# A banded attention with a feed-forward layer: value steps set directly ahead of score steps, and two tails woven into groups 3 and 5

## The chip, the cores and the metric

The kernel runs on one core of a Trainium2 chip. The metric is the device time of one execution in microseconds (us), taken as the median of several runs; lower is better. The engines of the core work through their own queues in program order and wait for each other through semaphores: PE (matmul, with PEld for the loads of its weights), DVE (vector), ACT (scalar), POOL (GpSimd) and SP, which only issues DMAs here.

## The reference

```python
# q, k, v: 8 batches x 8 heads x 576 positions x 64, float32
scores = q @ k^T / sqrt(64)
mask = (0 <= i - j) & (i - j < 64)          # a causal window of 64
attn = softmax(where(mask, scores, -1e9))
x = concat_heads(attn @ v)                  # 8 x 576 x 512
xn = (x - mean(x)) / sqrt(var(x) + 1e-6) * g_ln
out = x + relu(xn @ w_ch1) @ w_ch2          # w_ch1 512 x 2048, w_ch2 2048 x 512
```

All inputs and the output are float32; the kernel works with float16 operands in its matmuls.

## The kernel before, in words

The work is cut into nine groups. Groups 0 to 7 are positions 0 to 511 of one batch each, in four blocks (kb) of 128 positions. Group 8 holds the tails: positions 512 to 575 of all batches, two batches to a block, so four tail blocks, numbered by i. For each group the kernel does the feed-forward part (the MLP) of group g on PE while it prepares the attention of batch b = g + 1, loads and casts batch n = g + 2, and does one or two of the tails (TAILS: group 3 does tail 0, group 5 tail 1, group 7 tails 2 and 3).

The order is written out by hand. mlp_units returns a list of units, each a run of matmuls. Group 1 has 32 units: 16 of layer 1 (l1_half, L537, eight matmuls of 256 columns) and 16 of layer 2 (L413, four of 512). From group 2 on there are 30: units 0 to 15 are layer 1 (L401, four matmuls of 128x512 each), units 16 to 29 are layer 2 (L478, eight of 128x256 each: a Strassen-like scheme with seven products of two halves). In it DVE makes sums of the hidden layer (s_sums, L452). at(i, f, ...) puts a step into slot i, and the main loop emits unit i, then the steps of slot i in the order in which at was called. Since every engine's queue keeps the order of emission, a step's slot decides what stands ahead of it on each engine.

The steps of a block's attention are:

- cast_qk (L128, POOL) turns q or k of half a batch into float16. t_main then transposes it. From batch 3 on, q goes by a DMA transpose that SP issues (L223). k goes through PE (L229) and ACT, which copies the result to qkT (L215).
- s_mm (score step): 16 matmuls of 64 rows (L286) into two PSUM buffers sc; ACT takes their exponential (L294) into pt.
- s_mask: DVE multiplies pt by the window's mask (L301).
- b_step (value step): 16 matmuls of 64 columns (L321), which read pt and the float16 copies vA and vB of v, into the one buffer xps. DVE divides (L324, L327) and makes mean and variance (L329, L332, tile mvg).
- z_step: POOL normalises in four instructions (L351 to L354, tiles rsz and z). In groups 0 and 1 DVE does it instead, and newton (L380 to L390), a run of twelve small DVE instructions, makes the factors.
- zt_step: z is transposed to zT, the next MLP's input; mostly by a DMA that SP issues (L362), for block 3 of batches 3 and 5 by PE (L366).

For v, cast_v (L147, POOL) makes vA, and make_vB (L165, L166) copies it shifted by half a block with two DMAs that POOL issues. cast_tail (L117 to L120) and t_tail (L248, L257) do the like for a tail. The loads of batch n + 1 (load_qk L94, load_v L141) are issued by SP at the end of the group, those of a tail (load_tail, L106 to L108) in slot 1.

Buffers that matter here: two sc, one xps, two for PE's transposes, two for MLP sums (mm), two float16 buffers each for q and k, three z, four pt.

Before the change the steps of batch b in groups 2 to 6 sit in these slots: value steps 2, 7, 12, 17; score steps of blocks 1 to 3 in slots 2, 7, 12, each behind a value step; the score step of block 0 of batch n in slot 27. A tail of group 3 or 5 has its score step in slot 1, its value step in slot 5. In group 1 the score steps of batch 2 sit in 9, 13, 16, 19 and its value steps in 14, 17, 20, 23.

Of the kernel before, what the change touches and what calls it, by code (L numbers as in the profile page):

```python
# [20 lines left out]
def kernel(  # L21
# [11 lines left out]
    B, H, S, D = q.shape  # L33
# [3 lines left out]
    NGRP = B + 1  # L37
# [4 lines left out]
    XQ = 3  # L42
# [802 lines left out]
    TAILS = {3: [0], 5: [1], 7: [2, 3]}  # L845
    for g in range(NGRP):
        if g == NGRP - 1:
            for _ in rest:
                pass
            break  # L850
        units, s_sums = mlp_units(g, (8, 16)[g] if g < 2 else 0, g == 0, g > 1)
        slots = [[] for _ in range(len(units) + 1)]

        def at(i, f, *a):
            slots[min(i, len(slots) - 1)].append((f, a))

        b = g + 1
        if g == 0:
            at(0, b_step, 0, 3)
            at(1, zt_step, 0, 2)  # L860
            at(3, zt_step, 0, 3, "dve")
            at(4, newton, 0, 0, 4)
            at(11, t_main, 1, 0, 0, 1)
            at(12, t_main, 1, 1, 0, 1)
            at(13, vB_cur, 1, 0, 1)
            at(13, vB_prev, 1, 0, 1)
            at(13, vB_cur, 1, 1, 1)
            at(13, vB_prev, 1, 1, 1)
            at(16, s_mm, 1, 0)
            at(16, s_mask, 1, 0)  # L870
            at(17, s_mm, 1, 1)
            at(17, s_mask, 1, 1)
            at(18, b_step, 1, 0)
            at(20, b_step, 1, 1)
            at(21, zt_step, 1, 0)
            at(23, zt_step, 1, 1)
            at(24, t_main, 1, 0, 1, 0)
            at(26, t_main, 1, 1, 1, 1)
            at(25, vB_cur, 1, 2, 0)
            at(25, vB_prev, 1, 2, 1)  # L880
            at(26, vB_cur, 1, 3, 0)
            at(28, s_mm, 1, 2)
            at(28, s_mask, 1, 2)
            at(30, s_mm, 1, 3)
            at(30, s_mask, 1, 3)
            at(27, load_v, 2, 0, 4)
        if g == 1:
            at(0, cast_qk, 2, 0)
            at(0, cast_qk, 2, 1)
            at(0, b_step, 1, 2)  # L890
            at(2, b_step, 1, 3)
            at(3, zt_step, 1, 2)
            at(13, newton, 1, 0, 4)
            at(6, zt_step, 1, 3)
            at(4, alloc_v, 2)
            at(4, alloc_qkT, 2)
            at(4, alloc_vB, 2)
            at(5, cast_v, 2, 0, 4)
            at(5, make_vB, 2)
            at(4, t_main, 2, 0, 0)  # L900
            at(4, t_main, 2, 1, 0)
            at(6, t_main, 2, 0, 1)
            at(6, t_main, 2, 1, 1)
            at(7, w2_sums, 3, 0, 4)
            at(8, w2_sums, 3, 4, 8)
            at(25, w2_sums, 2, 0, 4)
            at(28, w2_sums, 2, 4, 8)
            for j in range(4):
                at((9, 13, 16, 19)[j], s_mm, 2, j)
                at((10, 14, 17, 20)[j], s_mask, 2, j)  # L910
                at((14, 17, 20, 23)[j], b_step, 2, j)
                at((14, 17, 20, 23)[j], z_step, 2, j)
                at((18, 21, 24, 27)[j], zt_step, 2, j)
            at(3, load_qk, 3, 0)
            at(4, load_qk, 3, 1)
            at(7, load_v, 3, 0, 4)
            at(8, alloc_qkT, 3)
            at(8, cast_qk, 3, 0)
            at(10, cast_qk, 3, 1)
            at(14, alloc_v, 3)  # L920
            at(14, cast_v, 3, 0, 2)
            at(14, cast_v, 3, 2, 4)
            at(17, alloc_vB, 3)
            at(17, make_vB, 3)
            at(31, s_mm, 3, 0)
            at(31, s_mask, 3, 0)
            for i, (x, half) in zip((12, 24, 12, 28), ((0, 0), (1, 0), (0, 1), (1, 1))):
                at(i, t_main, 3, x, half, 0)
            at(40, load_qk, 4, 0)
            at(40, load_qk, 4, 1)  # L930
            at(40, load_v, 4, 0, 4)
        if g == 2:
            for m, i in enumerate((1, 4)):
                at(4 + 2 * m, w2_sums, i, 0, 4)
                at(5 + 2 * m, w2_sums, i, 4, 8)
        if g > 1 and g + 2 < B:
            at(11, alloc_qkT, g + 2)
            if g + 2 >= XQ:
                at(11, cast_qk, g + 2, 0, (0,))
                at(11, cast_qk, g + 2, 1, (0,))  # L940
                at(11, cast_qk, g + 2, 0, (1,))
            else:
                at(11, cast_qk, g + 2, 0)
        if g > 1 and b < B:
            for j in range(4):
                if j:
                    at((2, 7, 12)[j - 1], s_mm, b, j)
                    at((3, 8, 13)[j - 1], s_mask, b, j)
                at((2, 7, 12, 17)[j], b_step, b, j)
                at((2, 7, 12, 17)[j], z_step, b, j)  # L950
                at((12, 12, 18, {3: 24, 5: 23}.get(b, 22))[j], zt_step, b, j)
        for n, i in enumerate(TAILS.get(g, ())):
            ts = (13, 13, 17, 22) if n else (1, 2, 5, 11)
            at(ts[0], s_mm, NGRP - 1, i)
            at(ts[1], s_mask, NGRP - 1, i)
            at(ts[2], b_step, NGRP - 1, i)
            at(ts[2], z_step, NGRP - 1, i)
            at(ts[3], zt_step, NGRP - 1, i)
        n = g + 2
        if g > 1 and n < B:  # L960
            at(16, cast_qk, n, 1, (1,) if n >= XQ else (0, 1))
            at(20, alloc_v, n)
            at(20, cast_v, n, 0, 2)
            at(21, cast_v, n, 2, 4)
            at(21, alloc_vB, n)
            at(21, make_vB, n)
            for i, (x, half) in zip((13, 18, 13, 22) if g == 2 else (13, 17, 13, 21),
                                    ((0, 0), (1, 0), (0, 1), (1, 1))):
                at(i, t_main, n, x, half, 0)
            at(27, s_mm, n, 0)  # L970
            at(28, s_mask, n, 0)
            if n + 1 < B:
                at(40, load_qk, n + 1, 0)
                at(40, load_qk, n + 1, 1)
                at(40, load_v, n + 1, 0, 4)
        if g > 1:
            for i in range(1, 5):
                at(7 + i, s_sums, 0, 4, i)
                at(13 + i // 3, s_sums, 4, 6, i)
                at((15, 15, 19, 21)[i - 1], s_sums, 6, 8, i)  # L980
        for n, i in enumerate(TAILS.get(g + 1, ())):
            if n == 0:
                at(1, load_tail, i)
                at(24 if i < 2 else 18, cast_tail, i)
                at(27 if i < 2 else 22, t_tail, i, 0)
                at(29 if i < 2 else 22, t_tail, i, 1)
            else:
                at(25, load_tail, i)
        if len(TAILS.get(g, ())) == 2:
            at(3, cast_tail, TAILS[g][1])  # L990
            at(7, t_tail, TAILS[g][1], 0)
            at(7, t_tail, TAILS[g][1], 1)
        if g == NGRP - 2:
            at(0, w1_sums, 1, 2)
            at(3, w1_sums, 3)
            at(21, w1_sums, 4)
            at(27, z_sums, NGRP - 1, 1, 2)
            at(28, z_sums, NGRP - 1, 3, 4)
            at(27, begin_last)
            at(28, lambda: next(rest))  # L1000
        for i, u in enumerate(units):
            if i == (20 if g > 1 else 17 if g == 0 else -1):
                tbank["shared"] = True
            u()
            for f, a in slots[i]:
                f(*a)
        for f, a in slots[len(units)]:
            f(*a)
# [28 lines left out]
```

## Time and profile before

| what | value |
|---|---|
| median of 3 runs | 308.82 us (308.48 to 309.07) |
| the profiled execution | 310.37 us |
| its span, first to last instruction | 308.5 us |
| mean granted TensorE clock | 0.999 |
| PE, DVE, POOL, ACT busy | 96%, 72%, 56%, 49% of the span |
| q1, the DMA queue of SP | 73% of 16 engines' span, 54.67 MB |
| group 1 starts its layer 1 at | 55.9 us |
| group 2 | 95.1 us |
| group 3 | 126.5 us |
| group 4 | 157.8 us |
| group 5 | 189.2 us |

The page of the profile gives each engine's busy time, then the span in 40 slices, the DMA queues, the chain of work that ended last, and groups of instructions by source line. Further views are answers of the trace: who waited for whom; the timeline, with start, length, engine, line, operation and tiles of each instruction or run of them, and in brackets the idle time ahead of it with its releaser; the instructions of one tile with the time from issue to landing of the DMAs that write it; and busy time in chosen stretches. SPq is SP's issue of a DMA; its length is that of the issue and not of the transfer. Starts are counted from the span's start. Matmuls overlap in the array, so the distance from one start to the next tells what one costs; its listed length is longer.

### The profile page before, as it was taken

How to read it: one execution, taken by the hardware profiler on the slowest of the kernel's cores; microseconds unless marked ns; L12 is line 12 of the kernel's file. 1: busy time of each engine (PE TensorE's matmuls, PEld its weight loads, DVE VectorE, ACT ScalarE, POOL GpSimd, SP SyncE). 2: the span in 40 equal slices, each digit the busy share in tenths (PEclk: the TensorE clock that was granted, in tenths of full speed). 3: DMA queues.
4: the chain of work that ended last, by engine and by line, in shares of the span. 5: the costliest groups of instructions: out<-in, count | busy, mean ns of one | idle time of the engine just before them, and what ended most of it. 6: DMA issues, size and time to landing. Idle time of an engine off the chain costs nothing.

```text
span 308.5 us, 7581 instructions
## 1 busy us (share of the span) xinstructions
PE 296.3 (96%) x3061; PEld 196.6 (64%) x3061; DVE 221.2 (72%) x412; ACT 150.8 (49%) x253; POOL 172.0 (56%) x256
## 2 busy tenths in 40 slices
PE   7989999997999999999999999999999999999992
PEld 4557544686454479646964686459645864788882
DVE  0688665767784996589666965897569686689972
ACT  1486635676316742775247526762376046305500
POOL 6588676536780798369814984598337507024300
PEclk9999999999999999999999999999999999999999
DMA  8999998999856997898479997994790399003014
GB/s 190 294 360 303 305 361 242 302 282 251 151 140 191 269 208 118 254 312 157 44 215 320 195 169 206 325 142 78 213 189 19 53 178 215 19 17 138 0 37 102
DMA packets 113669, 58.35 MB, mean 189 GB/s; under 512 B 83617, under 2 KB 104609, under 8 KB 113634
## 3 DMA queue, kind: packets, MB, share of 16 engines
q1 hardware_dynamic: 112576, 54.67, 73.1%
q0 software_dynamic: 768, 2.80, 3.8%
q8 instruction: 24, 0.39, 0.5%
q10 hardware_dynamic: 290, 0.40, 0.5%
q14 instruction: 11, 0.09, 0.1%
HBM read 38.80 MB, written 9.44 MB: 156 GB/s over the span
## 4 chain that ended last, share of the span: by engine, by line
PE 81%; DVE 5%; DMA 5%; POOL 3%; ACT 2%; issue 1%; SPq 1%; POOLq 0%; ACTq 0%
PE hps L401 25%; PE pA L478 10%; PE pC L478 7%; PE pB L478 7%; PE ch L413 5%; PE hph L537 4%; PE xps L321 4%; PE ch L554 3%; PE sc L286 3%; PE tp L229 3%; DMA v<-in_v_dram 3%; PE lA L592 2%; DMA zT<-z 2%; ACT pt L294 2%; PE warm L765 2%
## 5 line engine op out<-in xcount | busy, mean ns | idle before, releaser
L401 PE MATMUL hps<-zT,w1g 128*128 128x512 f16 x416 | 95.3, 379 | 0.0
L405 ACT ACTIVATE hrT<-hps 128x512 f16<-128x512 f32 x104 | 62.2, 599 | 39.4 <-PE hps L401 35.8
L401 PEld LDWEIGHTS <-w1g 128*128 128x128 f16 x416 | 38.6, 98 | 43.3 <-issue 0.7
L294 ACT ACTIVATE pt<-sc 128x512 f16<-128x512 f32 x72 | 39.0, 595 | 28.4 <-PE sc L286 19.9
L478 PEld LDWEIGHTS <-sS 128*128 128x128 f16 x448 | 43.3, 98 | 5.0
L351 POOL TENSOR_SCALAR rsz<-mvg 128x1 f32<-128x1 f32 x28 | 10.2, 363 | 63.9 <-DVE mvg L332 63.2
L128 POOL CAST qk<-qk 128x1024 f16<-128x1024 f32 x32 | 34.5, 1096 | 10.3 <-DMA qk<-in_q_dram 5.3
L301 DVE TENSOR_TENSOR pt<-pt,mask 128x1024 f16<-128x1024 f16 x32 | 28.9, 907 | 10.3 <-ACT pt L294 10.2
L478 PEld LDWEIGHTS <-hrT 128*128 128x128 f16 x336 | 32.4, 98 | 5.5 <-ACT hrT L637 0.3
L215 ACT COPY qkT<-tp 128x1024 f16<-128x1024 f16 x16 | 16.1, 1013 | 34.2 <-PE tp L229 34.1
L485 DVE TENSOR_TENSOR xn<-pA,xn 128x512 f32<-128x512 f32 x28 | 19.2, 685 | 16.8 <-PE pA L478 11.2
L478 PE MATMUL pC<-w2s,sS 128*128 128x256 f16 x224 | 27.1, 273 | 0.0
L478 PE MATMUL pA<-wT,sS 128*128 128x256 f16 x224 | 26.9, 273 | 0.0
L354 POOL TENSOR_SCALAR z<-xn,rsz 128x512 f16<-128x512 f32 x28 | 24.8, 885 | 3.0 <-DMA zT<-z 0.2
L329 DVE BATCH_NORM_STATS2 stats<-xn 128x6 f32<-128x512 f32 x36 | 25.0, 695 | 1.2
L327 DVE TENSOR_TENSOR xn<-xps,rcp 128x512 f32<-128x512 f32 x36 | 24.9, 691 | 1.2
L324 DVE RECIPROCAL rcp<-xps 128x8 f32<-128x8 f32 x36 | 7.3, 204 | 25.1 <-PE xps L321 25.1
L452 DVE TENSOR_TENSOR sS<-hrT 128x512 f16<-128x512 f16 (+1 forms) x40 | 24.5, 612 | 0.6 <-ACT hrT L405 0.6
L537 PE MATMUL hph<-zT,w1g 128*128 128x256 f16 x192 | 23.3, 273 | 0.5 <-DVE zT L371 0.5
L321 PEld LDWEIGHTS <-pt 128*64 128x64 f16 x576 | 12.3, 110 | 15.3 <-issue 6.8
L147 POOL CAST vA<-v 128x1024 f16<-128x1024 f32 (+2 forms) x19 | 17.3, 928 | 6.1 <-DMA v<-in_v_dram 6.0
L352 POOL TENSOR_TENSOR rsz<-rsz,mhalf 128x1 f32<-128x1 f32 x28 | 19.3, 691 | 2.3
(113 smaller groups left out, 450.1 us busy)
## 6 DMA issues: line engine op xcount, KB each, us to landing
out_dram<-xn SPq DMA_DIRECT2D x33, 256.0 KB, 2.4
qk<-in_q_dram SPq DMA_DIRECT2D x16, 512.0 KB, 6.3
qk<-in_k_dram SPq DMA_DIRECT2D x16, 512.0 KB, 7.2
v<-in_v_dram SPq DMA_DIRECT2D x32, 256.0 KB, 7.2
w2s<-in_moe_w_ch_dram SPq DMA_DIRECT2D x9, 512.0 KB, 9.2
w1s<-in_moe_w_ch_dram SPq DMA_DIRECT2D x4, 512.0 KB, 8.2
tk<-in_k_dram SPq DMA_DIRECT2D x8, 256.0 KB, 4.4
tv<-in_v_dram SPq DMA_DIRECT2D x8, 256.0 KB, 5.2
```

The lines of the kernel that those rows point to most:

```text
L128: nc.gpsimd.tensor_copy(out=dst[:, :].rearrange("p (a j) e d -> p a e j d", j=j), in_=t[:, :].rearrange("p (a e j d) -> p a e j d", e=2, j ...
L294: nc.scalar.activation(out=o, in_=i, func=AF.Exp, bias=0.0, scale=scale)
L301: nc.vector.tensor_tensor(out=ptv, in0=ptv, in1=mb, op=ALU.mult)
L321: nc.tensor.matmul(out=xps[64 * r:64 * r + 64, h, :D + 1], lhsT=pt[:, par, hp, r, :], rhs=rhs, start=True, stop=True)
L327: nc.vector.tensor_tensor(out=xn, in0=xps[:, :, 0:D], in1=rcp_b, op=ALU.mult)
L329: nc.vector.bn_stats(out=stats, in_=xv)
L354: nc.gpsimd.tensor_scalar(out=z, in0=xv, scalar1=rs, scalar2=nm, op0=ALU.mult, op1=ALU.add)
L401: nc.tensor.matmul(out=hps, lhsT=w1g[:, kc, 128 * hc:128 * (hc + 1)], rhs=zT[g][:, kc, :], start=(kc == 0), stop=(kc == NKC - 1),)
L405: nc.scalar.activation(out=hrT[:, hc, :], in_=hps, func=AF.Relu, bias=0.0, scale=1.0)
L452: nc.vector.tensor_tensor(out=o, in0=x, in1=y, op=op)
L478: nc.tensor.matmul(out=o, lhsT=a[:, c, 128 * p:128 * p + 128], rhs=wv[:, c, :], start=(first and (p == 0 or split_c) and c == 0), stop=(c ...
L537: nc.tensor.matmul(out=hps[:, e], lhsT=w1g[:, kc, 128 * hc:128 * (hc + 1)], rhs=zT[g][:, kc, 256 * half:256 * half + 256], start=(kc == 0) ...
```

## The change

It moves steps between slots. No instruction is added or removed.

- Group 1 (batch 2): newton from slot 13 to 9. Score steps to 10, 13, 15, 18, value steps to 15, 18, 21, 23. Those of blocks 0 and 1 now stand directly ahead of the score steps of blocks 2 and 3. The zt_steps go to 19, 22, 25, 27.
- Groups 3 and 5 (tails): value step of block 0 in slot 2, then the tail's score step; the tail's value step in slot 6, then the score step of block 1; value step 1 and score step 2 in slot 10; value step 2 and score step 3 in slot 14; value step 3 in slot 18. The tail's zt_step goes from 11 to 14, those of batch b from 12, 12, 18, 22 to 12, 15, 20, 23.
- Group 4: value step of block 3 from slot 17 to 19, and directly behind it the first score step of batch 6, from 27. So that it can stand there, the transposes of k of batch 6 are called in slots 16 and 17 (17 and 21 before) and the cast of k's second half in slot 13 (16 before). The zt_step of block 3 goes from 23 to 24.
- Groups 2, 6 and 7 keep their slots; group 7 alone keeps the old way of doing tails.

```diff
-            at(13, newton, 1, 0, 4)
+            at(9, newton, 1, 0, 4)
...
-                at((9, 13, 16, 19)[j], s_mm, 2, j)
-                at((10, 14, 17, 20)[j], s_mask, 2, j)
-                at((14, 17, 20, 23)[j], b_step, 2, j)
-                at((14, 17, 20, 23)[j], z_step, 2, j)
-                at((18, 21, 24, 27)[j], zt_step, 2, j)
+                at((15, 18, 21, 23)[j], b_step, 2, j)
+                at((15, 18, 21, 23)[j], z_step, 2, j)
+                at((10, 13, 15, 18)[j], s_mm, 2, j)
+                at((11, 14, 16, 19)[j], s_mask, 2, j)
+                at((19, 22, 25, 27)[j], zt_step, 2, j)
...
+        n = g + 2
         if g > 1 and b < B:
+            tails = g in TAILS and n < B
+            bs = (2, 10, 14, 18) if tails else (2, 7, 12, 19 if g == 4 else 17)
+            ss = (6,) + bs[1:3] if tails else bs[:3]
+            if tails:
+                i = TAILS[g][0]
+                at(bs[0], b_step, b, 0)
+                at(bs[0], z_step, b, 0)
+                at(bs[0], s_mm, NGRP - 1, i)
+                at(bs[0] + 1, s_mask, NGRP - 1, i)
+                at(ss[0], b_step, NGRP - 1, i)
+                at(ss[0], z_step, NGRP - 1, i)
+                at(14, zt_step, NGRP - 1, i)
             for j in range(4):
-                if j:
-                    at((2, 7, 12)[j - 1], s_mm, b, j)
-                    at((3, 8, 13)[j - 1], s_mask, b, j)
-                at((2, 7, 12, 17)[j], b_step, b, j)
-                at((2, 7, 12, 17)[j], z_step, b, j)
-                at((12, 12, 18, {3: 24, 5: 23}.get(b, 22))[j], zt_step, b, j)
-        for n, i in enumerate(TAILS.get(g, ())):
+                if j or not tails:
+                    at(bs[j], b_step, b, j)
+                    at(bs[j], z_step, b, j)
+                if j < 3:
+                    at(ss[j], s_mm, b, j + 1)
+                    at(ss[j] + 1, s_mask, b, j + 1)
+                at((12, 15 if tails else 12, 20 if tails else 18, {3: 24, 4: 23, 5: 24, 6: 23}.get(b, 22))[j], zt_step, b, j)
+        for n, i in enumerate(TAILS.get(g, ()) if g == NGRP - 2 else ()):
             ts = (13, 13, 17, 22) if n else (1, 2, 5, 11)
...
-            at(16, cast_qk, n, 1, (1,) if n >= XQ else (0, 1))
+            at(13 if g == 4 else 16, cast_qk, n, 1, (1,) if n >= XQ else (0, 1))
...
-            for i, (x, half) in zip((13, 18, 13, 22) if g == 2 else (13, 17, 13, 21),
+            for i, (x, half) in zip({2: (13, 18, 13, 22), 4: (13, 16, 13, 17)}.get(g, (13, 17, 13, 21)),
                                     ((0, 0), (1, 0), (0, 1), (1, 1))):
                 at(i, t_main, n, x, half, 0)
-            at(27, s_mm, n, 0)
-            at(28, s_mask, n, 0)
+            at(19 if g == 4 else 27, s_mm, n, 0)
+            at(20 if g == 4 else 28, s_mask, n, 0)
```

## The prediction

> **What bounds the kernel now.** I read the page first (busy shares, then the chain that ended last), then the waits of PE, then the timelines of PE, POOL and SP (its DMA queue) around each edit.
>
> ```profile
> PE 296.3 (96%) x3061; PEld 196.6 (64%) x3061; DVE 221.2 (72%) x412; ACT 150.8 (49%) x253; POOL 172.0 (56%) x256
> PE 81%; DVE 5%; DMA 5%; POOL 3%; ACT 2%; issue 1%; SPq 1%; POOLq 0%; ACTq 0%
> ```
>
> PE is the bound: 96% busy, 81% of the chain. A shift of PE work can therefore gain only by taking out a wait or an overhead of PE, and every new wait of PE costs its full length. PE's waits have one large entry:
>
> ```profile
> PE xps L321 <- DVE rstmp L387: 1.7, 1, 1.7
> ```
>
> It stands at 74.65 to 76.32, before the value step of batch 2, block 0. Its mask (L301) ended at 73.95 and nothing of L387 (newton) is an input of it; so the named releaser had no part in it. The tile vB, asked for alone around 66 to 72 us, shows another:
>
> ```profile
> L165 POOL DMA_DIRECT2D vB<-vA x1: 744/744/744, 68.9 to 68.9; - x1
> DMA to landing us min/median/max: 7.3/7.4/7.4
> ```
>
> 68.87 + 7.4 = 76.27: the wait ends with vB's landing. The median over all such copies is 3.0 to 3.7 us; this one runs beside four loads of v.
>
> PE's overhead is seen in its timeline in group 3 (start, length, line):
>
> ```profile
> 130.39 2.76 PE L401 MATMUL hps<-zT,w1g 128*128 128x512 f16 x12
> 133.09 0.45 PE L321 MATMUL xps<-vt,pt 128*64 128x65 f16 x16
> 133.47 1.90 PE L401 MATMUL hps<-zT,w1g 128*128 128x512 f16 x8
> ...
> 136.03 4.49 PE L401 MATMUL hps<-zT,w1g 128*128 128x512 f16 x20
> ...
> 140.83 0.41 PE L286 MATMUL sc<-qkT,qkT 64*128 64x64 f16 x16
> 141.17 2.76 PE L401 MATMUL hps<-zT,w1g 128*128 128x512 f16 x12
> ```
>
> Twelve L401 take 133.09 - 130.39 = 2.70, twenty take 4.42 (to the value step at 140.45): 0.215 each, and about 0.11 is left over, each time before another array shape. A value step (128*64) takes 0.38 from its start to the next one's, a score step (64*128) 0.34. Value, then score directly: 140.45 to 141.17, 0.72, with no second 0.11 between.
>
> [...] the mask L301 takes 0.66 alone and 1.45 at 142.73 beside a cast; POOL's L353 takes 0.26 alone and 0.88 at 139.35 beside the sums of L452. [...] Here the stretch after the last matmul, 303.0 to 308.5, has a mean clock of 0.94, the only lower one; no inner gap is over 1.7 us[...].
>
> **The change part by part** (times are those of the trace before, each group counted from its own start).
>
> Fewer changes of shape. Groups 3 and 5 have seven visits to the small shapes before and six after; group 4 five and four; group 1, from slot 9 on, nine and seven. 5 x 0.10 = -0.5 us. The number of matmuls, of DVE, ACT and POOL instructions and of DMAs is unchanged.
>
> Batch 2, block 0, one unit later. PE arrives 0.87 us later (one unit of eight L537) while vB lands at 76.27 as before, as everything ahead of it on POOL and SP is in the same order. Of 1.7 us about 0.85 goes: -0.85 us. newton's twelve small DVE instructions now stand ahead of the mask of block 0. They would start at 69.7; casts occupy POOL from 70.39 to 74.85[...]. If one gets in per cast, the mask ends near 76; bounds 74 and 77, so between 0 and +0.7. I take 0, since vB's landing covers it; if vB came sooner the whole would show. Also in group 1 POOL now casts v of batch 3 ahead of z of block 0, and makes vB of batch 3 ahead of z of block 1. z of block 3 then ends near 91.3 (91.98 before), its transpose lands 2.7 us later, about 94.1, and group 2 would start at 94.0: I take +0.1, bounds 0 and 0.7.
>
> Groups 3 and 5: tails woven in. The value step of block 1 moves from unit 7 to unit 10, on PE from 135.30 to 137.73 (units 7 to 10 behind a score step at 133.85). On POOL its z stands ahead of the three casts of the next q and k:
>
> ```profile
> 137.76 0.54 POOL L351 TENSOR_SCALAR rsz<-mvg 128x1 f32<-128x1 f32 x1 [0.15 <-DVE mvg L332]
> 141.62 3.46 POOL L128 CAST qk<-qk 128x1024 f16<-128x1024 f32 x3
> ```
>
> z starts as its mvg comes and the casts follow at once: from 137.76 to 145.08 without a pause. PE transposes the third cast's tile (L229) at 145.99, a margin of 0.9. After the change z starts 2.43 later, so the casts end at 145.08 + 2.4 = 147.5, a little earlier if DVE's sums collide less, 147.3. PE comes to L229 sooner, at 145.3, as the value step of block 3 no longer stands ahead of it in that slot. Wait: 2.0 us, bounds 0.1 (no collisions at all: z 2.1 instead of 3.7 us, the casts 3.0 instead of 3.5) and 2.4. Nothing else takes PE's time there. Two groups: +4.0 us. What follows (second cast of k, z of block 3, vB) has 0.6 us or more of margin after this. On SP the transposes of z of the tail and of block 1 move behind those of the next q; the work that hides them is units 15 to 29, as their first reader is the next group (tail: group 8), and without it each would cost its 1.2 us of issue.
>
> Group 4: the first score step of batch 6 from unit 27 to unit 19, and k's transposes from 17 and 21 to 16 and 17. POOL's order stays: three casts, z of block 2, the cast of k's second half. PE's lines, POOL's lines and SP's, and the landing of the two DMAs of L223:
>
> ```profile
> 174.14 1.91 PE L478 MATMUL pA<-w2s,hrT 128*128 128x256 f16 x16
> ...
> 186.32 0.41 PE L286 MATMUL sc<-qkT,qkT 64*128 64x64 f16 x16
> 186.74 0.40 PE L248 MATMUL tpq<-ident,tq 128*128 128x128 f16 x4
> ```
>
> ```profile
> 172.00 3.46 POOL L128 CAST qk<-qk 128x1024 f16<-128x1024 f32 x3
> ...
> 178.25 1.03 POOL L128 CAST qk<-qk 128x1024 f16<-128x1024 f32 x1
> ```
>
> ```profile
> 176.29 3.21 SPq L362 DMA_TRANSPOSE zT<-z  x2
> 179.60 2.72 SPq L223 DMA_TRANSPOSE qkT<-qk  x2
> ```
>
> ```profile
> DMA to landing us min/median/max: 4.8/4.8/4.8
> ```
>
> Stage units take 0.87. PE ends unit 16 at 175.0 and waits for the third cast until 175.5; transposes (0.45), unit 17, and at 176.8 waits for the last cast until 179.3 (2.5 us). Transposes, two units, the value step of block 3: 182.0. Now the score step, whose q comes through the DMA transposes. SP's order ahead of them is unchanged: the loads of batch 6 and of tail 1 (until 176.1), two of z, then these at 179.60 and 180.94. The second lands at 180.94 + 4.8 = 185.7. PE starts the second half of the scores then, against 182.0: another 3.7. It is through at 186.05, and has units 20 to 27 (8 x 0.87) and the transposes of z (0.22) to do before L248: 193.2, against 186.74. That is +6.5, or +6.6 without the saved change of shape counted above. Bounds: 5.2 if the landing takes 3.5, the median of all ten, and 7.6 if it takes one more. Before, the same landing was hidden behind units 20 to 27, with 0.6 to spare. The stall gives POOL time: z of block 3, the casts of v and of the tail end near 191, still ahead of 193.2. Groups 2, 6, 7 and 8 are moved as wholes.
>
> Sum: -0.5 - 0.85 + 0.1 + 4.0 + 6.6 = +9.35 us. The profiled execution took 310.37 around a span of 308.5 and would take 319.7; it stands 1.55 above the median of 308.82, to which I refer: 318.2.
>
> **The rivals.** (1) Only group 4 waits: the casts of groups 3 and 5 come in time because z meets fewer DVE sums. Then 318.2 - 4.0 = 314.2. For it: z of the tail, which meets no sums, takes 2.06 (135.55 to 137.61). Against: in the new order the sums of units 8 to 11 and a mask still fall on z of block 1, those of units 13 and 14 on the casts. (2) The clock drops in group 4, where PE is idle for 6.7 of 11 us. At half clock for a few us PE loses 2 to 4: 321. [...] Against: the first landing, at 184.4, lets eight score matmuls through in the longer one, and at the end of the kernel the fall came late: a mean of 0.94 over 5.5 us is 0.66 us at half clock, so it began near 307.8, about 4.6 us after the last matmul. (3) Faster: the transposes of q are in place when PE comes, and the casts too; then -0.5 - 0.85 + 0.1, 307.6. Its mechanism is that the feeds run ahead of PE rather than just in time; it decides from a landing at 182.0 or earlier, 3.7 before the one seen. The landings of 3.2 in other groups speak for it; the queue ahead of the two, loads until 176.1, speaks against, as nothing in it moves.
>
> **How the numbers follow.** Forecast, all three waits: 0.60, 318.2, own range 316.4 to 320. Rival 1: 0.18. Rival 2: 0.12. Rival 3: 0.05. Waits of group 4 cut to about 1 to 2 us, with the others: 0.03, slower too. Gains and losses that cancel: 0.02. Leaving 0.05 + 0.02 below and part of rival 2 above: 313.4 to 321.4. About 0.2% is what a measurement can tell from no change: faster 0.05, same 0.02, slower 0.93.
>
> **What would show it.** PE's waits after: L286 of batch 6 for the DMA of qkT, several us; L229 for POOL's L128 four times, 2 us in groups 3 and 5 and 0.5 and 2.5 in group 4; L321 at batch 2 down to about 0.85. PE idle 2 us in groups 3 and 5 and near 6.5 in group 4. It would be wrong if L223 lands before PE asks, or if POOL's casts end before 145.3 on the scale of group 3.

## The result, and the profile after

The changed kernel takes 319.54 us (median of 4 runs, 319.28 to 321.29) beside 308.68 of the kernel before (4 runs, 308.48 to 309.07): a ratio of 1.0362, 95% interval 1.0324 to 1.0401. The profiled execution took 319.28 us around a span of 317.4. It is slower, by 10.9 us where the prediction had 9.4. Of each kernel a few executions lie 1.5% or more above its fastest; the ratios in this document are formed without them.

The page of the changed kernel, busy times and chain that ended last:

```profile
PE 298.1 (94%) x3061; PEld 197.8 (62%) x3061; DVE 220.6 (70%) x412; ACT 151.1 (48%) x253; POOL 173.2 (55%) x256
PE 76%; POOL 8%; SPq 5%; DVE 3%; DMA 3%; ACT 2%; issue 1%; POOLq 0%; ACTq 0%
```

The instructions of the engines are as many as before. PE is busy 1.8 us longer and the span is 8.9 longer, so about 7 us are new idle time of PE (the 1.8 are mostly matmuls at half clock, see below), and the chain now runs through POOL and SP's queue. The waits of PE name them (engine, line, waited for: us in total, times, longest):

```profile
PE tp L229 <- POOL qk L128: 5.6, 4, 2.3
...
PE sc L286 <- DMA qkT<-qk: 1.8, 2, 1.2
PE hps L401 <- DMA zT<-z: 1.6, 1, 1.6
```

The 1.7 us at L321 in batch 2 are gone. In their place stand four waits for a cast, two for the DMA transposes of q, and one for the last zT at the start of group 2. Where each group starts (its first matmul of layer 1, from the two timelines), and what the group before it has gained or lost:

| start of | before | after | step |
|---|---|---|---|
| group 2 | 95.08 | 94.44 | -0.64 |
| group 3 | 126.52 | 125.80 | -0.08 |
| group 4 | 157.82 | 158.63 | +1.53 |
| group 5 | 189.16 | 196.56 | +6.59 |
| group 6 | 220.47 | 229.39 | +1.52 |

From group 6 on the steps are as before. The timeline of group 3 shows POOL's casts and PE's transposes (start, length, line; in brackets the idle time and its releaser):

```profile
142.87 3.38 POOL L128 CAST qk<-qk 128x1024 f16<-128x1024 f32 x3
```

```profile
146.31 0.62 PE L229 MATMUL tp<-ident,qk 128*128 128x128 f16 x8 [1.45 <-POOL qk L128]
```

The casts end at 146.25 and PE starts the moment they do. Group 4 has four such places on PE; after them SP's issues and the landing of the two DMAs of L223:

```profile
176.32 0.62 PE L229 MATMUL tp<-ident,qk 128*128 128x128 f16 x8 [0.34 <-POOL qk L128]
...
180.15 0.62 PE L229 MATMUL tp<-ident,qk 128*128 128x128 f16 x8 [2.33 <-POOL qk L128]
...
183.53 0.29 PE L286 MATMUL sc<-qkT,qkT 64*128 64x64 f16 x8 [0.64 <-DMA qkT<-qk]
...
185.03 0.29 PE L286 MATMUL sc<-qkT,qkT 64*128 64x64 f16 x8 [1.21 <-DMA qkT<-qk]
185.25 3.24 PE L478 MATMUL pA<-wT,sS 128*128 128x256 f16 x16
```

```profile
176.90 3.21 SPq L362 DMA_TRANSPOSE zT<-z  x2
180.21 2.63 SPq L223 DMA_TRANSPOSE qkT<-qk  x2
```

```profile
DMA to landing us min/median/max: 3.2/3.3/3.4
```

The brackets understate the gaps, since a matmul's end is modelled (the eight L229 at 176.32 list 0.62 us, and the next run starts 0.46 behind their start). From the distance of the starts, less what the matmuls before take without a wait, the four are 0.5, 2.5, 0.7 and 1.4: 5.1 us. The last line of PE shows something else: sixteen L478 take 3.24, against 1.91 for a run of sixteen in the profile before. The windows of the changed kernel give the reason (stretch, its length, busy time of PE, PEld, DVE, ACT and POOL, then PEclk, DMA share and GB/s):

```profile
182.20:185.60 3.40, 1.56 (x39) 1.06 (x38) 2.68 (x6) 0.26 (x1) 0.40 (x2) 1.00 0.77 148
185.70:189.00 3.30, 3.30 (x18) 2.34 (x16) 1.16 (x2) 0.72 (x2) 3.10 (x6) 0.50 0.03 7
```

PE had half its clock from 185.66 to 189.07, directly after a stretch in which it was busy for 1.56 of 3.40 us. From 185.25 to the start of group 5 this kernel takes 11.31 us; the same matmuls take 9.63 in an experiment below that keeps its clock. So group 4 lost 5.1 us to waits and 1.7 to the clock, and won about 0.2 at the changes of shape: 6.6.

### The profile page after: what moved, and what is told of

Same layout as the page of the kernel before. It is cut to its first block, busy times and chain, and to the rows that moved or that the text cites. A ratio compares the mean times of both kernels' runs of the same rounds, so it can differ in the third digit from the quotient of the medians.

```text
span 317.4 us, 7580 instructions
## 1 busy us (share of the span) xinstructions
PE 298.1 (94%) x3061; PEld 197.8 (62%) x3061; DVE 220.6 (70%) x412; ACT 151.1 (48%) x253; POOL 173.2 (55%) x256
## 4 chain that ended last, share of the span: by engine, by line
PE 76%; POOL 8%; SPq 5%; DVE 3%; DMA 3%; ACT 2%; issue 1%; POOLq 0%; ACTq 0%
PE hps L401 22%; PE pA L478 10%; PE pC L478 8%; PE pB L478 7%; PE hph L537 7%; PE xps L321 3%; PE ch L554 3%; PE sc L286 3%; PE tp L229 3%; SPq L141 2%; POOL qk L128 2%; PE lA L592 2%; POOL z L354 2%; PE ch L413 2%; PE warm L765 2%
## 5 line engine op out<-in xcount | busy, mean ns | idle before, releaser
L401 PE MATMUL hps<-zT,w1g 128*128 128x512 f16 x416 | 95.0, 380 | 1.6 <-DMA zT<-z 1.6
L401 PEld LDWEIGHTS <-w1g 128*128 128x128 f16 x416 | 38.7, 97 | 45.5 <-issue 2.8
L351 POOL TENSOR_SCALAR rsz<-mvg 128x1 f32<-128x1 f32 x28 | 11.7, 418 | 69.6 <-DVE mvg L332 68.9
L478 PEld LDWEIGHTS <-sS 128*128 128x128 f16 x448 | 44.1, 100 | 5.8
L128 POOL CAST qk<-qk 128x1024 f16<-128x1024 f32 x32 | 35.8, 1132 | 12.4 <-DMA qk<-in_k_dram 6.5
L478 PEld LDWEIGHTS <-hrT 128*128 128x128 f16 x336 | 32.1, 98 | 5.5 <-ACT hrT L637 0.3
L301 DVE TENSOR_TENSOR pt<-pt,mask 128x1024 f16<-128x1024 f16 x32 | 26.6, 831 | 9.7 <-ACT pt L294 9.7
L478 PE MATMUL pA<-wT,sS 128*128 128x256 f16 x224 | 28.4, 281 | 0.0
L478 PE MATMUL pC<-w2s,sS 128*128 128x256 f16 x224 | 27.5, 275 | 0.0
L452 DVE TENSOR_TENSOR sS<-hrT 128x512 f16<-128x512 f16 (+1 forms) x40 | 22.8, 571 | 0.6 <-ACT hrT L405 0.6
L321 PEld LDWEIGHTS <-pt 128*64 128x64 f16 x576 | 12.2, 110 | 13.4 <-issue 6.6
```

The source lines that it names most:

```text
L128: nc.gpsimd.tensor_copy(out=dst[:, :].rearrange("p (a j) e d -> p a e j d", j=j), in_=t[:, :].rearrange("p (a e j d) -> p a e j d", e=2, j ...
L301: nc.vector.tensor_tensor(out=ptv, in0=ptv, in1=mb, op=ALU.mult)
L321: nc.tensor.matmul(out=xps[64 * r:64 * r + 64, h, :D + 1], lhsT=pt[:, par, hp, r, :], rhs=rhs, start=True, stop=True)
L401: nc.tensor.matmul(out=hps, lhsT=w1g[:, kc, 128 * hc:128 * (hc + 1)], rhs=zT[g][:, kc, :], start=(kc == 0), stop=(kc == NKC - 1),)
L452: nc.vector.tensor_tensor(out=o, in0=x, in1=y, op=op)
L478: nc.tensor.matmul(out=o, lhsT=a[:, c, 128 * p:128 * p + 128], rhs=wv[:, c, :], start=(first and (p == 0 or split_c) and c == 0), stop=(c ...
```

## The experiments

Times are medians of each run's repetitions. The ratios are to runs of the kernel before made alongside, with a 95% interval; the kernel before had a median of 308.7 to 309.2 there. A ratio need not be the quotient of the two medians. "In the profile" means one execution of each kernel.

**The three parts alone.** Edits: the diff shown above, its lines for group 1, for groups 3 and 5, or for group 4 only.

> Only the part in group 1 is changed (score steps, value steps and newton of batch 2). Theory (the wait for vB goes, but the later z of block 3 lets the first matmul of group 2 wait for zT): the 1.7 us wait at L321 of batch 2 is gone, a wait of 1.6 to 1.8 us stands at the first L401 of group 2, and about 0.6 us are saved: 308.1. Rival 1 (the zT wait comes from the other parts or from chance in the loads): no zT wait, 2.4 us saved: 306.3. Rival 2 (the part is worth nothing by itself): 308.7, within 0.2.

> Only the part in groups 3 and 5 is changed (tail steps woven in between the blocks, z of block 1 ahead of three casts). Theory (a wait of L229 for the third cast in each of the two groups, 1.6 us each): +3.0 us, 311.7, with two waits of 1.5 us at L229 for POOL L128 and no others. Rival (the wait in group 5 is a consequence of what group 4 delayed, so that only group 3 pays here): +1.5, 310.2.

> Only the part in group 4 is changed (transposes of k and q of batch 6 and its first score step moved forward). Theory (waits for the casts and for the DMA transposes of q, 5.2 us, and about 1.6 us for the clock that is halved after them): +6.6, 315.3, with half clock for some 3.4 us once. Rival (the half clock belongs to the sum of all gaps since group 3, so that group 4 alone keeps the full clock): +5.0, 313.7. Second rival (the parts interact: batch 6's loads come earlier when group 3 isn't delayed, and the waits shrink to under 3 us): under 311.7.

| part alone | us | ratio | groups changed, in the profile |
|---|---|---|---|
| group 1 | 309.78 | 1.0042 (1.0018 to 1.0066) | wait for zT 1.8 |
| groups 3 and 5 | 311.82 | 1.0101 (1.0082 to 1.0121) | +1.52 and +1.52 |
| group 4 | 314.70 | 1.0154 (1.0094 to 1.0215) | +5.76 |

The medians stand 1.0, 3.1 and 6.0 us above that of the kernel before, together 10.1: most of the 10.9, so within the intervals the parts add up. Groups 3 and 5 cost what was expected, and group 5 pays by itself. Group 4 (whose medians alone give 1.019, inside the interval) stands at 6.0 between the 6.6 of the theory and the 5.0 of its rival; its profile has the half clock for 3.41 us once, which the rival denied, but shorter waits at L286 (1.2 us listed, against 1.8). Group 1 was a miss: expected 0.6 us faster, it is 1.0 slower, and yet the wait for zT stands as expected in its profile:

```profile
PE hps L401 <- DMA zT<-z: 1.6, 1, 1.6
```

The other kernels tell why, as the group 1 of several is that of the kernel before. From one and the same matmul of group 1 (at 63.95 in the profile before) to the first of group 2 it took:

| group 1 as before | us | group 1 changed | us |
|---|---|---|---|
| the profile before | 31.13 | the changed kernel | 30.86 |
| group 4 alone | 29.38 | group 1 alone | 30.87 |
| groups 3 and 5 alone | 30.10 | loads of the tail late (below) | 31.18 |
| group 4 mended (below) | 29.38 | filled waits (below) | 29.61 |
| k's cast in slot 9 (below) | 29.43 | | |
| three casts in slot 9 (below) | 29.68 | | |
| groups 3 to 5 mended (below) | 29.38 | | |

The vB wait of 1.7 us is not a fixed feature of the kernel before. It comes and goes with the execution: counted from that same matmul, the first of vB's two copies (L165) landed after 9.1 to 12.6 us in the fourteen profiles of this document, and PE is there after 10.5 us with the old group 1 and 11.4 with the changed one. In the profile before it landed after 12.2, with the whole wait, which accounts for its 310.37 us, 1.55 over the median; in the changed kernel after 10.3, too soon for a wait in the old order as well. An execution of that kind has nothing to gain from the later value step, and the wait for zT is pure loss.

**Group 4: which feed is late.** First the loads of tail 1 behind q's transposes on SP:

```diff
-                at(1, load_tail, i)
+                at(14 if g == 4 else 1, load_tail, i)
```

> The changed kernel with the loads of the tail of group 4 put behind the DMA transposes of q on SP (slot 14 instead of 1). Theory (L286 of batch 6 waits for q's transposes because SP issues them only after the last cast and the two zT transposes; the tail's loads aren't what delays them): wait at L286 stays at about 2.2 us, 319.3. Rival (the tail's loads stand ahead on SP or in the DMA engines and delay q's transposes): wait at L286 gone or under 0.5, and with fewer gaps perhaps the half clock too: 317.2, or 315.7 if the clock holds.

318.23 us (4 runs), ratio 1.0254 (1.0188 to 1.0319; the medians alone give 1.031). My theory falls, and the rival's mechanism holds, though the time is 1.0 above its 317.2: no wait at L286 is left. SP issues the transposes at 176.0 instead of 180.2:

```profile
176.01 2.62 SPq L223 DMA_TRANSPOSE qkT<-qk  x2
```

The six loads of the tail took SP from 170.9 to 176.7 in the changed kernel, ahead of z's transposes and q's (first and last of them):

```profile
170.85 1.15 SPq L106 DMA_DIRECT2D tq<-in_q_dram  x1
...
175.91 0.83 SPq L108 DMA_DIRECT2D tv<-in_v_dram  x1
```

That queue was the delay, and not the cast. Group 4 lost 4.61 instead of 6.59, with no half clock (PEclk 1.00 from 176 to 194). Not all of the saving stays: the tail's own cast stands behind z of block 3 on POOL and ends no sooner than in the changed kernel (192.5 against 192.0), and PE, which now comes earlier, meets it next:

```profile
PE tpq L248 <- POOL tq L118: 1.2, 1, 1.2
```

Then the clock. Seventeen matmuls of no use (identity by mask, into the two score buffers, read by nobody) fill the two longest waits:

```diff
+            if g == 4:
+                at(17, fill, 10)
...
+            if g == 4:
+                at(19, fill, 7)
             at(19 if g == 4 else 27, s_mm, n, 0)
```

> The changed kernel with 17 matmuls of no use set into the two longest waits of group 4 (ten ahead of the second transposes of k, seven ahead of the first score step of batch 6; 512 columns each, 0.215 us). Theory (the half clock follows from idle time of PE within a stretch of 3.4 us, so a PE that is kept busy keeps its clock): no half clock inside, about 1.6 us less: 317.9. Rival (the half clock has another cause, or the matmuls come on top of the waits instead of inside them): 319.5 or more, up to 323 if all 3.7 us come on top.

319.61 us (316.77 to 320.71 in only 4 runs), ratio 1.0311 (1.0254 to 1.0369). By the whole time the kernel is no faster than the changed one (319.54), which is the rival's figure and not the theory's 317.9. The stretch speaks for the theory: group 4 lost 4.83 in the profile, which is of the fastest of the four executions, against 6.59, and PE keeps its clock through it.

```profile
183.00:187.00 4.00, 3.90 (x45) 2.91 (x43) 2.83 (x7) 1.08 (x2) 2.41 (x6) 1.00 0.24 51
187.00:191.00 4.00, 4.00 (x41) 3.61 (x39) 2.08 (x4) 0.59 (x1) 4.00 (x8) 1.00 0.08 19
```

From the first L478 of group 4 to the one behind the score step of batch 6 the two kernels take the same time, 10.31 us in the changed one and 10.23 here, so the added matmuls lie inside the waits. The rest of the group takes 11.31 and 9.63: 1.7 us won by the clock. So more work in place of idle time made this group shorter, in one profile. The other three executions have no profile. Two of them had a mean granted clock of 0.998 and 0.999, against 0.989 to 0.991 in the four of the changed kernel. One step of 3.41 us at half clock takes 0.005 off the mean, so the clock was kept there too; what cost them 2.4 us and more over the profiled one stays open.

Last, group 4 with all its feeds moved ahead (groups 1, 3 and 5 as before the change; the lines of group 4 against those of the changed kernel):

```diff
-            at(11, alloc_qkT, g + 2)
-            if g + 2 >= XQ:
+            at(6 if g == 4 else 11, alloc_qkT, g + 2)
+            if g == 4:
+                at(6, cast_qk, 6, 0, (0,))
+                at(6, cast_qk, 6, 1, (0,))
+                at(11, cast_qk, 6, 0, (1,))
+            elif g + 2 >= XQ:
...
-            bs = (2, 10, 14, 18) if tails else (2, 7, 12, 19 if g == 4 else 17)
+            bs = (2, 10, 14, 18) if tails else (2, 7, 12, 17)
...
-            at(13 if g == 4 else 16, cast_qk, n, 1, (1,) if n >= XQ else (0, 1))
+            at(11 if g == 4 else 16, cast_qk, n, 1, (1,) if n >= XQ else (0, 1))
...
-            for i, (x, half) in zip({2: (13, 18, 13, 22), 4: (13, 16, 13, 17)}.get(g, (13, 17, 13, 21)),
+            for i, (x, half) in zip({2: (13, 18, 13, 22), 4: (11, 15, 11, 16)}.get(g, (13, 17, 13, 21)),
...
-            at(19 if g == 4 else 27, s_mm, n, 0)
+            at(17 if g == 4 else 27, s_mm, n, 0)
...
-                at(1, load_tail, i)
+                at(14 if g == 4 else 1, load_tail, i)
```

> Group 4 changed alone, in another way: casts of q in slot 6 and of k in slot 11, DMA transposes of q in slot 11, transposes of k in 15 and 16, first score step of batch 6 in slot 17 directly behind the value step of block 3 (which keeps its slot), loads of tail 1 behind q's transposes in slot 14. Theory (the score step can be had early if its feeds are moved ahead too): waits of group 4 under 0.5 us together, 308.7. Rival (the casts wait for the loads of q, hold up z and the casts of k, and PE waits for those): 1.5 to 3 us, 310.2 to 311.7.

309.16 us, ratio 1.0005 (0.9985 to 1.0025), as the theory had it: the four waits of group 4 are gone. It loses 0.11 all the same, since PE now waits 0.27 us for the tail's cast ahead of L248. The early score step was never the trouble; its inputs were.

**Groups 3 and 5: the cast ahead of z.** All three casts into slot 9, in the kernel with these groups changed alone:

```diff
-            at(11, alloc_qkT, g + 2)
+            e = 9 if g in TAILS else 11
+            at(e, alloc_qkT, g + 2)
             if g + 2 >= XQ:
-                at(11, cast_qk, g + 2, 0, (0,))
-                at(11, cast_qk, g + 2, 1, (0,))
-                at(11, cast_qk, g + 2, 0, (1,))
+                at(e, cast_qk, g + 2, 0, (0,))
+                at(e, cast_qk, g + 2, 1, (0,))
+                at(e, cast_qk, g + 2, 0, (1,))
```

> Groups 3 and 5 changed alone, and there the three casts of q and k put into slot 9, ahead of z of block 1, where POOL is idle for 1.4 us. Theory (L229 waits only since z of block 1 stands ahead of the casts): no wait at L229, both groups as long as before less 0.1 each; 308.5 beside 308.7 of the kernel before, within 0.2 per cent of it, and 3.3 us under the run with tails alone. Rival (the casts are late[...], whatever the order): 1.0 us or more of wait stays in each, 310.8.

310.89 us, ratio 1.0060 (1.0038 to 1.0082); each group loses 0.88 instead of 1.52. Neither theory is whole. The wait at L229 is gone, so its cause is the order on POOL; but a new one has come, for the mask of block 2. DVE, POOL and PE in group 3 of this kernel:

```profile
138.88 1.47 DVE L452 TENSOR_TENSOR sS<-hrT 128x1024 f16<-128x1024 f16 x1
140.27 1.52 DVE L301 TENSOR_TENSOR pt<-pt,mask 128x1024 f16<-128x1024 f16 x1
```

```profile
137.78 3.46 POOL L128 CAST qk<-qk 128x1024 f16<-128x1024 f32 x3
```

```profile
141.84 0.22 PE L321 MATMUL xps<-vB,pt 128*64 128x65 f16 x1 [0.91 <-DVE pt L301]
```

A sum and the mask take 1.47 and 1.52 beside the casts. The same two with no cast beside them, in the kernel with groups 3 and 5 alone:

```profile
138.24 0.66 DVE L452 TENSOR_TENSOR sS<-hrT 128x1024 f16<-128x1024 f16 x1
138.82 0.68 DVE L301 TENSOR_TENSOR pt<-pt,mask 128x1024 f16<-128x1024 f16 x1
```

Each took more than twice as long beside the casts. Since L229 reads k's first half only, one cast is enough ahead of z:

```diff
-                at(11, cast_qk, g + 2, 0, (0,))
-                at(11, cast_qk, g + 2, 1, (0,))
-                at(11, cast_qk, g + 2, 0, (1,))
+                at(9 if g in TAILS else 11, cast_qk, g + 2, 0, (1,))
+                at(11, cast_qk, g + 2, 0, (0,))
+                at(11, cast_qk, g + 2, 1, (0,))
```

> Groups 3 and 5 changed alone, and there the cast of k's first half alone put into slot 9, the two casts of q in slot 11 behind z of block 1. Theory (L229 needs this one cast only, and one cast of 1.0 us fits into POOL's 1.4 us of idle time without holding up the mask of block 2 as three did): no wait at L229 and under 0.3 us at L321 in each group; each as long as before less 0.1; level with the kernel before. Rival (any cast there collides with DVE's sums and mask, and z of block 1 then does): 0.5 to 0.9 us in each, 1 to 2 us in all.

308.48 us, ratio 0.9966 (0.9941 to 0.9990). In these groups there is no wait at L229 and none over 0.1 us at L321, and each of the two groups is 0.07 shorter than before. The one cast and the mask now miss each other:

```profile
136.93 1.04 POOL L128 CAST qk<-qk 128x1024 f16<-128x1024 f32 x1
```

```profile
138.86 0.69 DVE L301 TENSOR_TENSOR pt<-pt,mask 128x1024 f16<-128x1024 f16 x1
```

The two groups gain 0.14 us, but group 4 of the same profile is 0.14 longer (PE waits there for z of block 3), so the profile accounts for none of the 0.34%. In the two kernels that build on this one, below, the ratio is 0.9991; I take the 0.34% for spread.

**Group 1: why zT is late.** The casts of v of batch 3 and its copy moved back on POOL, with group 1 changed alone: first to slots 16 and 19 (behind z of blocks 0 and 1), then to 23 and 24 (behind all four z).

```diff
-            at(14, alloc_v, 3)
-            at(14, cast_v, 3, 0, 2)
-            at(14, cast_v, 3, 2, 4)
-            at(17, alloc_vB, 3)
-            at(17, make_vB, 3)
+            at(16, alloc_v, 3)
+            at(16, cast_v, 3, 0, 2)
+            at(16, cast_v, 3, 2, 4)
+            at(19, alloc_vB, 3)
+            at(19, make_vB, 3)
```

The second kernel has 23 in place of 16 and 24 in place of 19.

> Group 1 changed alone, and there the casts of v of batch 3 and the copy of it put behind z of blocks 0 and 1 on POOL, as before the change. Theory (zT is late at the start of group 2 because of these 5 us of POOL work ahead of z): the 1.6 us wait at L401 is gone or under 0.3; 1.5 us under the run with group 1 alone, 308.3, level with the kernel before (which on most executions has little of the vB wait). Rival (zT is late because z of block 3 follows value step 3, which is in the same slot as before, and POOL has time enough): the wait stays, 309.8.

> Group 1 changed alone, and there v of batch 3 cast in slot 23 and its copy made in slot 24, behind all four z of batch 2 on POOL. Theory (from the first value step of batch 2 POOL works without a pause up to z of block 3, and this row of 12 us sets the start of group 2): with 3.7 us of it gone the wait for zT at L401 is under 0.4 us, against 1.6 with the group alone and 0.7 with the casts behind z of blocks 0 and 1; 0.3 to 0.5 us under the latter, 308.7. Rival (zT of block 3 is late by SP's queue or its landing, not by POOL): 0.7 us or more stays. Third possibility: the first value step of batch 3 waits for vB, which is now asked for last; up to 2 us more, 310.7.

First kernel: 309.09 us, ratio 1.0005 (0.9986 to 1.0024), 0.9 us of the wait left, between the two theories. Second: 308.40 us, ratio 0.9991 (0.9970 to 1.0012), no wait at L401. So POOL's row of work, from the first value step of batch 2 to z of block 3, sets zT. With group 1 alone that row also held a wait: the cast of v's second half stood ahead of z of block 0 and had to wait for its load, with z's input ready since 77.

```profile
79.23 1.04 POOL L147 CAST vA<-v 128x1024 f16<-128x1024 f32 x1 [1.53 <-DMA v<-in_v_dram]
```

In the changed kernel this wait is 1.34 us. How much of the 1.8 is this load and how much the casts and the copy, the runs don't separate, since both kernels here move the casts behind z of block 0. In the first kernel that row runs without a pause from 77.4 to 90.8, and with zT's transpose behind it is 0.9 us longer than PE's own way to group 2. The second takes 3.7 us out, and POOL pauses ahead of each z. Its profile shows instead a wait for vB again, at the later slot too:

```profile
PE xps L321 <- DMA vB<-vA: 0.9, 1, 0.9
```

**What works, together.** Groups 3 to 5 mended with group 1 as before, and group 1 (second kernel) with groups 3 and 5 mended and group 4 as before:

> Group 1 as in the kernel before, groups 3 and 5 with the cast of k's first half in slot 9, group 4 with its feeds moved ahead as in the run that did this alone: all pairs of value and score step of groups 3 to 5 without the waits. Theory (three changes of array shape fewer are all that there is to gain): 0.3 us under the kernel before, which the measurement can hardly tell from nothing: 308.5 to 309. Rival (the pairs take pressure from other queues as well): 307.5 or less.

> Group 1 changed as in the run with v of batch 3 cast in slots 23 and 24, groups 3 and 5 as in the run with the cast of k's first half in slot 9, group 4 as in the kernel before. Theory (the pairs save four changes of array shape, 0.4 us, and the first value step of batch 2 has one unit more of cover for vB, worth 0 to 0.9 us with the execution): no wait at L401 of group 2, none at L229; 308.0 to 308.7 beside about 309.1 of the kernel before, a ratio of 0.997 to 0.999. Rival (what each gains alone was the spread of the executions): ratio 1.000.

The first takes 308.96 us, ratio 0.9991 (0.9966 to 1.0016), the second 308.49, ratio 0.9991 (0.9971 to 1.0010). The pairs are to be had without waits, and are then worth what three or four shape changes are worth: nothing that was measured with certainty. The profiled execution of the second took 311.71, and shows a risk that the prediction had bounded, newton ahead of the mask. DVE, POOL and PE's wait in group 1 of it:

```profile
70.34 3.61 DVE L381 TENSOR_SCALAR rstmp<-rstmp 128x4 int32<-128x4 int32 x1
```

```profile
70.92 4.16 POOL L128 CAST qk<-qk 128x1024 f16<-128x1024 f32 x4
```

```profile
PE xps L321 <- DVE pt L301: 1.7, 1, 1.7
```

One tiny instruction of newton (0.17 us in the changed kernel) took 3.61 us here, and four casts ran beside it and after it from 70.92 to 75.08 without a gap: POOL had waited for v until 67.19 (64.12 in the changed kernel, where the same four casts are spread from 68.26 to 76.35), and all four halves of q and k were there. That the casts held it is read from the times alone: it ended at 73.95, and the third of them near 74.0. The mask of block 0 stands behind newton on DVE and came 1.9 us late for PE; vB, which landed near 76.4, would have accounted for 1.1 of that. A half clock followed (columns as above):

```profile
75.00:78.30 3.30, 1.55 (x39) 0.99 (x37) 3.02 (x13) 1.24 (x3) 0.07 (x1) 1.00 1.15 198
78.40:81.80 3.40, 3.40 (x10) 1.20 (x9) 1.68 (x4) 0.71 (x2) 1.75 (x4) 0.50 1.09 172
```

## Why the prediction was right, and which terms were mis-sized

**What bounds, and the sign: right.** PE is the bound, each new wait of PE cost its length, and the waits stand at the lines foretold: L229 four times, L286 in batch 6. That the sum came within 1.5 us is in part luck: errors of opposite sign stand behind it.

**Fewer shape changes, -0.5: not contradicted.** Without waits the two tail groups gained 0.07 each, of 0.1 foretold, by their profile; no measured time resolves it.

**Batch 2, block 0, -0.85, and the reference to the median: wrong.** The step took the saving off the profiled execution and then put the result 1.55 us lower, because the profiled execution "stands 1.55 above the median". Both are the same 1.7 us: four of the six other profiles with the old group 1 have no such wait, and the remaining two 0.3 and 0.6 us of it. Against the median this term is 0, not -0.85.

**zT at the start of group 2, +0.1 with bounds 0 and 0.7: wrong.** It measured 1.8 us in the changed kernel. z of block 3 ended at 91.9 in a profile whose group 1 runs 0.4 earlier, so 1.0 later than the 91.3 foretold; the row on POOL had in it 1.3 us of waiting for v's load, which the step left out. And PE came sooner: with no vB wait at all, and two shape changes fewer, it was through at 92.65. The step had PE arrive with its wait half kept. The bound of 0.7 left out that PE's way and POOL's row lengthen and shorten apart. These two terms are the largest error: group 1 was to bring about 0.95 with its shape changes and costs 1.0 as a part alone.

**newton ahead of the mask, taken as 0, bounds 0 and 0.7: right in the changed kernel** (the mask of block 0 ended at 73.7, sooner than the 74 to 77 given). One instruction of newton per cast was my estimate; three of the twelve took 0.88 to 1.00 us there, each of them started while a cast ran, and the other nine 0.16 or 0.17. The upper bound was real: about 0.8 us more than vB in the last profile.

**Groups 3 and 5, +4.0: right mechanism, too large.** Each wait is 1.6 us, so 3.2. z of block 1 did start 2.5 us later; but it took 3.1 us where 3.7 had been the old one's, with 2.9 us of DVE's sums and masks beside it in place of 3.4, and the casts ended at 147.0 on the scale of the prediction instead of 147.3.

**Group 4, +6.6: right sum, two errors that cancel.** The waits for the casts are 0.5 and 2.5 as foretold. The wait for q's transposes is 2.1, not 3.7: they landed in 3.3 us and not in 4.8 as in the profile before. What had been seen once was taken for a property of the place. The missing 1.6 came from the clock (1.7), which is rival 2, and it acted on top of a shorter wait. Rival 2's price (2 to 4) was a little high; the doubt set against it, that the longer gap is broken by eight matmuls, is answered below. Rival 1 and rival 3 are ruled out for this order by the four waits at L229; rival 3's mechanism, feeds ahead of PE, is what the mended kernels do.

In sum: against the median, group 1 was put about 2 us too low, groups 3 and 5 some 0.8 too high, and group 4 was right by accident. That is 1.2 of the 1.5 us between the forecast and the result.

## What to carry to other kernels

Moving a consumer earlier pays only if each of its feeds, on every queue that it passes through, moves far enough ahead to be in place; look for the queue that is in no dependency of yours (here six loads of a tail on SP, and z's four instructions on POOL). Before a wait in a profile is counted as a gain, set that execution's time against the median: if it lies above by the length of the wait, the median probably doesn't have it. A merged pair saves about 0.1 us of PE here, so it can't pay for a wait of even 0.2.

## What the runs showed that was not expected

In these traces the clock changed on a grid. The half clock inside lasted 3.41 us each time (185.66 to 189.07 in the changed kernel), and every stretch at full clock between two changes is a whole number of 3.413 us: 296.96 in the profile before (87), 126.29 in the changed kernel (37), 129.71 in group 4 alone (38), 68.27 and 225.28 in the last kernel (20 and 66). The traces also show how much PE was idle ahead of a half clock. I laid the grid over fourteen traces and summed PE's gaps in each step (own sums, from the distances of the starts):

| step of the grid, kernel | PE idle in it | next step |
|---|---|---|
| 175.53 to 178.94, group 4 alone | 2.44 us | half clock |
| 182.25 to 185.66, changed kernel | 2.36 us | half clock |
| 74.96 to 78.37, last kernel | 2.10 us | half clock |
| 90.77 to 94.19, group 1 alone | 1.90 us | full |
| 144.70 to 148.11, changed kernel | 1.80 us | full |
| 175.42 to 178.83, changed kernel | 1.69 us | full |

All other inner steps have 1.7 us or less and none is followed by half clock. The steps in which a kernel's last matmul falls agree: with 2.45 us (first group 1 kernel with later casts of v) and 2.39 us (filled waits) idle, the next step was at half clock (mean granted clock 0.995 in both executions); with 2.04 us (loads of the tail late) and 1.96 us (the second such group 1 kernel) it was not (0.999 in both). In these traces the border lies between about 2.0 and 2.1 of 3.4 us, in one gap or in several, if every matmul, transposes too, counts as work: the 2.36 us of the changed kernel hold the gaps of 0.7 and 1.4 ahead of and behind eight score matmuls. The same gap of 2.5 us in group 4 fell into one step in one kernel (2.44) and was split over two in the other (1.2 of the 1.69, and the rest after it), with and without half clock behind it. One step of 3.41 us at half clock, with PE at work all through it, cost 1.7 us in group 4. No run was made to find the border itself.
